# Chunk 2's first layer by half products, chunk 1's second layer in two-bank running sums, and one written order from chunk 0's tail on

## The chip, the cores and the metric

The kernel runs on one core of a Trainium2 chip. Five engines work side by side, each on its own list of instructions: PE (TensorE, matmuls into PSUM), DVE (VectorE) and ACT (ScalarE), which read and write PSUM and SBUF, POOL (GpSimd, SBUF alone), and SP (SyncE), which issues most DMAs. The metric is device time in microseconds; smaller is better. Times of the kernel before are three runs, 273.68 to 274.18, median 273.87.

## The reference

An attention without softmax feeds a layer with an activation. For each of 8 batches and 8 heads, with 576 positions and 64 features:

```python
def phi(x, c, s):                      # c, s: cos and sin of (pi/2) * pos / S
    r = np.maximum(x, 0.0)
    return np.concatenate([r * c, r * s], axis=-1)
q_p, k_p = phi(q, cos_w, sin_w), phi(k, cos_w, sin_w)
kv  = einsum('bhsf,bhsd->bhfd', k_p, v)
num = einsum('bhsf,bhfd->bhsd', q_p, kv)
den = einsum('bhsf,bhf->bhs', q_p, k_p.sum(axis=2))[..., None] + 1e-6
x   = (num / den) as 4608 tokens x 512
h   = x @ w_in                         # 512 x 2048
out = (h / (1 + exp(-beta * h))) @ w_out   # 2048 x 512, fp32
```

Inputs and output are fp32 in HBM; the matmuls take bf16.

## The kernel before

**Tiles and stages.** The 4608 tokens are nine chunks of 512 (eight blocks of 64); the attention comes in eight batches of nine blocks, so batch 2, say, fills chunk 2's last six blocks and chunk 3's first three. For each batch: `load_raw` (L79, on SP) brings q, k and v, 1.15 MB each, into one buffer per name, so that a load waits until the batch before has been read. `q_relu`, `k_relu` (L193 on DVE or L192 on ACT) and `v_scale` (L219 on DVE or L217 on ACT; nine instructions each for cos and for sin) make bf16 operands. `q_turn_dma` (L259) turns q by a DMA on SP, and `tan_mul` (L223, DVE or POOL) makes its sine half. `kv_mm` (L276) and `kv_take` (L286) make kv; `num_all` (L297) makes num for three blocks; `x_div` (L308, L312, L319, all DVE) divides; `x_turn_dma` (L367, SP) turns x into the chunk's `xt`.

**First layer (h).** It has 16 groups of 128 features. `h_group` is four wide matmuls (512 columns, L386) into one bank, and a Silu on ACT (L394) that writes bf16 `g_t`. Chunks 0, 1 and 2 do this. From chunk 3 on, `h_pair` takes two groups at a time as a 2x2 block product with seven half-size products instead of eight (Winograd's form): each product is two narrow matmuls (256 columns, L511) with sums of weights (`wh_sum`, L443) or of x (`x_sum`, L455) as operands. `fast_ops` keeps running sums in two halves of two PSUM banks: a seed copy on ACT (L480), a kept copy (L484, ACT or DVE) and adds on DVE (L487); Silu is L420.

**Second layer (output).** Chunk 0 takes `o_mm`: 64 wide matmuls (L544), four copies (L550), stores by POOL (L537). Chunk 1 takes `o_fast` (L563): seven products of eight narrow matmuls for each half of the tokens, three banks a half, copies L602 to L604 and L582 on ACT, adds L606 to L608 on DVE. Chunks 2 to 8 take `o_pair` (L621), the same seven products through `fast_ops`. The operands are the sums S1 to S4 of `g_t` (`g_sum`, L406, DVE) and T1 to T4 of w_out (`w_sums`, L876 to L879, DVE, 128x2048 each).

**What sets the order.** `manual_schedule` is on: each engine runs its instructions in the order in which the code emits them, and waits by semaphores. Chunk 0, its 32 slots and the work hung into them (`early`), chunk 1 and the first layer of chunk 2 (`h_first`) are loops and lines in the code; from chunk 2's second layer on the order is a string per chunk, `ORDERS`, one word an instruction or a small group (for example `h25` is product 5 of pair 2, `oxd` a kept copy of the output's half x, `s21` a g sum, `w4` a scale on DVE, `v4` one on ACT).

**Around the change.** Slot 27 is the twelfth of chunk 0's sixteen output slots; loads of batch 2 are issued in slot 24. After slot 31, chunk 1's loop (16 `h_group`s) carries `num_rest`, ReLUs, scales and the kv of batch 2 and `w_sums`; then come lines with `o_fast`, batch 2's num in one block (`for t, bank in enumerate((4, 6, 0)): num_all(2, t, bank)`) between the first product of each half and the rest; then `h_first(2)` with batch 3's work and eight w_in sums, and `chunk(2)`.

Of the kernel before, what the change touches and what calls it, by code (L numbers as in the profile page):

```python
# [22 lines left out]
def kernel(  # L23
# [384 lines left out]
    def g_sums(c, i0, i1):  # L408
        for kind in (1, 3, 2, 4):
            got = g_sum(c, i0, i1, kind)  # L410
        return got
# [10 lines left out]
    def wx_tiles():  # L422

        wx["w"] = stage.tile([P, 4, 512], FP32, name="w_stage", tag="w_stage").rearrange("q a f -> q (a f)").bitcast(
            BF16).rearrange("q (k s g f) -> q k s g f", k=4, s=4, g=2)
        wx["v"] = stage.tile([P, 4, 512], FP32, name="w_stage", tag="w_stage").rearrange("q a f -> q (a f)").bitcast(
            BF16).rearrange("q (k s g f) -> q k s g f", k=4, s=4, g=2)
        wx["x"] = stage.tile([P, 4, 512], FP32, name="w_stage", tag="w_stage").rearrange("q a f -> q (a f)").bitcast(
            BF16).rearrange("q (s n c) -> q s n c", s=8, n=NB // 2)
        wx["q"] = stage.tile([P, 4, 512], FP32, name="w_stage", tag="w_stage").rearrange("q a f -> q (a f)").bitcast(  # L430
            BF16)[:, 0 : 2 * NQ * P].rearrange("q (s n c) -> q s n c", s=2, n=NQ)

    def w_sum(jt, i):
        return wx["w" if jt % 4 == 0 else "v"][:, jt // 4, i]

    def wh_sum(jt, kind):
        f0 = jt % 4
        A11, A12, A21, A22 = (win[jt // 4][:, 2 * jp : 2 * jp + 2, f * P : (f + 1) * P]
                              for f in (f0, f0 + 1) for jp in range(2))
        s1, s2, s3, s4 = (w_sum(jt, i) for i in range(4))  # L440
        o, l, r, op = {1: (s1, A21, A22, ALU.add), 2: (s2, s1, A11, ALU.subtract),
                       3: (s3, A11, A21, ALU.subtract), 4: (s4, A12, s2, ALU.subtract)}[kind]
        return nc.vector.tensor_tensor(o, l, r, op=op)  # L443

    def wh_sums(jt):
        for kind in (1, 3, 2, 4):
            got = wh_sum(jt, kind)
        return got
# [55 lines left out]
    def h_pair(c, i):  # L504
# [16 lines left out]
        s1, s2, s3, s4 = (w_sum(jt0, k_) for k_ in range(4))  # L521
# [269 lines left out]
    def second():  # L791
# [22 lines left out]
        28: lambda: x_turn_pe(1, 0, 7, 4, ("act",), (0,)),  # L814
        29: lambda: x_turn_pe(1, 0, 7, 5, ("dve",), (1,)),
    }

    def num_rest():
        for n in range(7, NQ):
            for jp in range(2):  # L820
                num_mm(1, n, jp, 2, 2 * (n - 7) + jp)
        x_mul(x_rden(2, 0, 7, NQ, (0, 1)), 7, NQ)
        x_turn_dma(1, 7, NQ)

    def att_q(b, turn=True):
        q_relu(b, 0)
        q_relu(b, 1)
        if turn:
            q_turn_dma(b)
        if b + 1 < B and b != 3:  # L830
            load_raw(b + 1, "q")

    def v_half(b, cs, n0=0, n1=NQ, eng="dve"):
        if b >= B:
            return
        v_scale(b, cs, n0=n0, n1=n1, eng=eng)
        if cs == 1 and n1 == NQ and b + 1 < B:
            load_raw(b + 1, "v")

    def k_all(b):  # L840
        k_relu(b)
        if b + 1 < B:
            load_raw(b + 1, "k")

    def kv_all(b, bank=6, eng="dve"):
        kv_mm(b, 0, bank)
        kv_mm(b, 1, bank)
        kv_take((0, 1), bank, eng)
# [5 lines left out]
    for slot in range(32):  # L854
# [26 lines left out]
    wx_tiles()  # L881
    for slot in range(16):
        h_group(1, slot)
        if slot == 0:
            num_rest()
            att_q(2)
            v_half(2, 0)
        if 2 <= slot < 6:
            v_half(2, 1, slot + 3, slot + 4, "act")
        if slot == 4:  # L890
            k_all(2)
            v_half(2, 1, 0, 5)
        elif slot == 6:
            w_sums()
        elif slot == 10:
            kv_all(2, eng="act")
            for jp in range(2):
                tan_mul(nc.vector, qs_of(2)[:, jp], qts[0][:, jp], 0, NQ)
    q_relu(3, 0, "act")
    q_relu(3, 1, "act")  # L900
    q_turn_dma(3)

    def one_sums(kind):
        for i0 in range(0, JT // 2, 2):
            g_sum(1, i0, i0 + 2, kind)

    def ops(of, names):
        for n in names.split():
            of[n]()

    x, y = o_fast(1, 0, (2, 5, 4)), o_fast(1, 1, (3, 7, 6))
    ops(x, "1 c1")
    one_sums(1)
    ops(y, "1 c1")
    for t, bank in enumerate((4, 6, 0)):
        num_all(2, t, bank)
    one_sums(2)
    x_part(2, 0, 4)
    ops(x, "6 cu")
    ops(y, "6 cu")  # L920
    one_sums(3)
    ops(x, "2 5 c5")
    x_part(2, 1, 6)
    ops(x, "7")
    one_sums(4)
    ops(x, "a2 a7")
    ops(y, "7 2")
    got = wh_sums(0)
    x_part(2, 2, 0)
    load_raw(4, "q")  # L930
    q_tan(3, 0, got)
    q_tan(3, 1)
    ops(y, "a2 5 c5")
    ops(x, "3 a3 4 c4")
    ops(y, "a7 3 a3 4 c4")
    v_half(3, 0)

    ORDERS = {
        2: (
            "ox16 W61 N12 N00 oy17 x0 oxc4 oyc5 ox5 ox6 oxd k2 k0 k3 k1 v5 x1 N20 oxe W62 oy6 v4 v1 v3 oy5 Lk x2 oyD "  # L940
            "oye v0 ox7 q1 q0 w2 w8 ox3 ox2 oy3 w1 w3 oy7 w7 oy2 v7 w5 w6 oyf w4 oxf oy4 v8 W64 ox4 oyX W63 v6 oyB w0 "
            "t1 t3 t2 v2 oxA t4 Lv Lq oxB"),
        3: (
            "W51 h012 TQ h213 K00 h2c5 W11 h0c7 K1 h22 kT h05 h25 h06 h26 h0d h02 h2d W31 h110 h15 h311 h1c4 h0e h35 "
            "h2e W12 h07 W13 h0f W32 h27 h03 h1d h3d h2f h3c6 h23 h0A W52 h2A h12 W14 h04 W71 h36 W33 W72 h24 h16 h517 "
            "h1e W34 h0B h32 h3e h615 h2B h55 h13 h712 h75 h5D h37 h1A h33 h5c3 h3f h17 h3A h7D h65 h52 h1f h7c4 h6D "
            "g0 h34 h56 h5e h416 W54 W73 h3B h14 h6c1 h76 h72 h1B h45 h53 h4c0 W53 h4d h62 W74 h57 h66 h7e h73 h5A h6e "
            "h5f h77 g1 h42 h7A v7 h46 h7f h4e h67 h63 h54 h6f w2 h74 h6A h47 h43 h4A N03 h64 h5B oy11 h7B h4f h6B h44 "
            "ox10 h4B s11 s30 w4 x0 w6 s10 oyc7 N13 N25 s13 oxc2 s12 s20 v6 v8 k0 ox5 oxd s22 k3 ox2 oy5 w5 v1 s21 k1 "
            "s23 s32 ox6 v2 v3 x1 s31 oxe oyd s42 s40 s41 oy2 oy6 s43 w8 w3 ox3 s33 oye ox7 oy3 q1 v4 v0 w1 w7 k2 Lk "  # L950
            "w0 oy7 oxf v5 oyf ox4 t1 oy4 x2 oxB Lv oyY oxA q0 Lq t2 oyA t4 t3"),
# [38 lines left out]
            "oy6 oy2 oxd s42 s43 s41 oxe s40 oye ox3 oxA ox7 oxf oy7 oyU oyf ox4 oxY oy4 oy3 oyB oyV"),  # L990
    }

    def chunk(c, last):
        b = c + 1
        pairs = {f"h{i}": h_pair(c, i) for i in range(JT // 2)} if c > 2 else {}
        pairs.update({"ox": o_pair(c, 0), "oy": o_pair(c, 1)})
# [95 lines left out]
```

## Time and profile before

| what | value |
|---|---|
| median of 3 runs | 273.87 us (273.68 to 274.18) |
| span of the profiled execution | 272.7 us |
| median less span | 1.2 us |
| PE / DVE / ACT / POOL busy | 97% / 82% / 69% / 25% of the span |
| matmuls | 3712 |
| HBM read and written | 36.71 MB and 9.44 MB |

The page takes one execution. "Busy" adds up the time in which an engine has an instruction in flight; for PE, matmuls overlap, so the distance from one start to the next tells more than the duration (a 256-column matmul lasts 272 ns in its row and the next one starts 109 ns later). The same holds for DVE and ACT to a lesser degree (an add lasts 428 ns and the next starts 336 ns after it). "Idle before" is time in which an engine stood still ahead of a group, with what ended it.

Where the stages lie, by the PE timeline and the chain: chunk 0's second layer 31.9 to 50.4 us (with batch 1's kv and num), chunk 1's first layer to 66 us, its second to 80.6 us, chunk 2's first layer to 95.7 us, its second to 109.7 us; from then on a chunk takes some 27.5 us while batches are in work and 24.5 us without. In four stretches the engines are busy as follows:

| stretch, us | PE | DVE | ACT | POOL |
|---|---|---|---|---|
| 47.5 to 69.0 (21.5) | 21.50 | 17.57 | 16.86 | 4.74 |
| 69.0 to 80.6 (11.6) | 10.64 | 10.11 | 3.23 | 4.09 |
| 80.6 to 95.7 (15.1) | 15.10 | 14.13 | 11.96 | 7.17 |
| 95.7 to 109.7 (14.0) | 14.00 | 12.40 | 8.22 | 0.46 |

### The profile page before, as it was taken

The page shows a single profiled execution, that of the slowest core. Times are in us where ns is not written, and L with a number is a line of the kernel's source. Part 1 is how long each engine was busy: PE and PEld are TensorE (multiplying, and loading weights), DVE is VectorE, ACT ScalarE, POOL GpSimd, SP SyncE. Part 2 cuts the span into 40 slices and gives each one's busy share as a digit, 9 for nine tenths or more (in the row PEclk, how much of TensorE's full clock was granted, in tenths as well). Part 3 has the DMA queues.
Part 4 walks back from the last instruction along what each step waited for, and adds up shares of the span by engine and source line. Part 5 has one row for each costly group of instructions (what it writes and reads, how often), then busy time and mean ns, then how long its engine had stood idle before and what let it go on. Part 6 is the DMA issues. An engine that isn't in the chain of part 4 may idle for free.

```text
span 272.7 us, 8970 instructions
## 1 busy us (share of the span) xinstructions
PE 265.3 (97%) x3712; PEld 206.8 (76%) x3712; DVE 224.0 (82%) x596; ACT 188.4 (69%) x384; POOL 68.3 (25%) x89
## 2 busy tenths in 40 slices
PE   8899999999899999999999999999999999999994
PEld 8554455455784588888888888888888888888883
DVE  5989969499989889789989997899589768757852
ACT  4778777796419656899489966996696179428920
POOL 1444000510078000660085009300840060000001
PEclk9999999999999999999999999999999999999999
DMA  6999999999969999994589439943600570015005
GB/s 237 374 395 383 392 390 319 379 201 336 284 130 311 240 348 226 240 313 103 147 216 370 92 58 223 332 71 62 181 2 2 61 185 1 2 27 130 0 2 155
DMA packets 50681, 54.00 MB, mean 198 GB/s; under 512 B 31232, under 2 KB 31760, under 8 KB 50640
## 3 DMA queue, kind: packets, MB, share of 16 engines
q1 hardware_dynamic: 47504, 45.55, 59.1%
q0 software_dynamic: 2784, 7.61, 9.6%
q8 instruction: 29, 0.48, 0.7%
q10 hardware_dynamic: 352, 0.27, 0.4%
q14 instruction: 12, 0.10, 0.1%
HBM read 36.71 MB, written 9.44 MB: 169 GB/s over the span
## 4 chain that ended last, share of the span: by engine, by line
PE 85%; DVE 9%; DMA 3%; SPq 1%; issue 1%; ACT 1%; DVEq 0%
PE ps L621 32%; PE ps L511 27%; PE ps L386 10%; PE ps L544 5%; PE ps L563 4%; PE ps L297 3%; DMA raw_v<-in_v_dram 3%; PE ps L276 3%; DVE vb L219 1%; DVE xs L319 1%; DVE qs L223 1%; SPq L79 1%; DVE S L406 1%; DVE rk L193 1%; DVE qb L193 0%
## 5 line engine op out<-in xcount | busy, mean ns | idle before, releaser
L537 POOL DMA_DIRECT2D out_dram<-o_sb x58 | 33.9, 591 | 147.3 <-ACT o_sb L658 86.3
L420 ACT ACTIVATE g_t<-ps,beta 128x512 bf16<-128x512 f32 x96 | 60.3, 702 | 1.4 <-PE ps L511 1.3
L621 PEld LDWEIGHTS <-S 128*128 128x128 bf16 x448 | 43.4, 98 | 5.2
L511 PE MATMUL ps<-w_stage 128*128 128x256 bf16 x288 | 46.6, 272 | 0.1
L386 PE MATMUL ps<-xt,win 128*128 128x512 bf16 (+1 forms) x196 | 42.8, 375 | 0.1
L511 PEld LDWEIGHTS <-w_stage 128*128 128x128 bf16 x384 | 37.3, 98 | 5.1 <-issue 0.2
L487 DVE TENSOR_TENSOR ps<-ps,p 128x256 f32<-128x256 f32 x74 | 30.5, 428 | 8.6 <-PE ps L511 3.0
L394 ACT ACTIVATE g_t<-ps,beta 128x512 bf16<-128x512 f32 x48 | 32.3, 688 | 7.2 <-PE ps L386 7.1
L621 PEld LDWEIGHTS <-g_t 128*128 128x128 bf16 x336 | 32.3, 98 | 4.5 <-ACT g_t L420 0.4
L386 PEld LDWEIGHTS <-win 128*128 128x128 bf16 x196 | 18.7, 98 | 21.1 <-issue 0.5
L511 PE MATMUL ps<-xt,win 128*128 128x256 bf16 x192 | 32.9, 273 | 0.0
L511 PEld LDWEIGHTS <-win 128*128 128x128 bf16 x288 | 28.0, 98 | 3.4
L621 PE MATMUL ps<-wout,g_t 128*128 128x256 bf16 x224 | 28.9, 273 | 0.0
L406 DVE TENSOR_TENSOR S<-g_t 128x512 bf16<-128x512 bf16 (+1 forms) x66 | 25.7, 418 | 3.3 <-ACT g_t L420 1.7
L480 ACT COPY ps<-ps 128x256 f32<-128x256 f32 x62 | 22.6, 383 | 7.5 <-PE ps L621 4.0
L217 ACT ACTIVATE vb<-raw_v,sin 128x256 bf16<-128x256 f32 (+1 forms) x58 | 26.0, 503 | 1.5 <-DMA raw_v<-in_v_dram 1.5
L621 PE MATMUL ps<-T,S 128*128 128x256 bf16 x224 | 26.6, 273 | 0.0
L621 PE MATMUL ps<-wout,S 128*128 128x256 bf16 x224 | 26.4, 273 | 0.0
L319 DVE TENSOR_TENSOR xs<-ps,rden 128x768 bf16<-128x768 f32 (+4 forms) x26 | 22.8, 884 | 0.9 <-DVE rden L312 0.2
L223 POOL TENSOR_TENSOR qs<-qt,tanr 128x1152 bf16<-128x1152 bf16 x6 | 14.3, 2387 | 27.4 <-PE ps L563 21.0
L658 ACT COPY o_sb<-ps 128x512 f32<-128x512 f32 x11 | 6.3, 587 | 20.1 <-PE ps L621 20.1
L487 DVE TENSOR_TENSOR ps<-ps,u 128x256 f32<-128x256 f32 x36 | 15.3, 427 | 5.3 <-PE ps L511 3.3
(112 smaller groups left out, 414.7 us busy)
## 6 DMA issues: line engine op xcount, KB each, us to landing
raw_v<-in_v_dram SPq DMA_DIRECT2D x7, 1152.0 KB, 9.7
raw_k<-in_k_dram SPq DMA_DIRECT2D x7, 1152.0 KB, 9.5
raw_q<-in_q_dram SPq DMA_DIRECT2D x7, 1152.0 KB, 7.4
out_dram<-o_sb POOLq DMA_DIRECT2D x58, 128.0 KB, 4.5
w_stage<-in_moe_w_in_dram SPq DMA_DIRECT2D x3, 1024.0 KB, 12.8
w_stage<-in_moe_w_out_dram SPq DMA_DIRECT2D x2, 1024.0 KB, 7.9
w_stage<-in_moe_w_out_dram SPq DMA_DIRECT2D x4, 512.0 KB, 11.9
out_dram<-o_sb SPq DMA_DIRECT2D x10, 128.0 KB, 2.4
```

What stands on the lines that cost most here:

```text
L217: got = nc.scalar.activation(o, a, AF.Copy, scale=t[:, n : n + 1])
L223: return eng.tensor_tensor(dst.rearrange("q n (g p) -> q n g p", g=2), src.rearrange("q n (g p) -> q n g p", g=2), tanr[:, n0:n1].unsqueez ...
L319: nc.vector.tensor_tensor(o.rearrange("q j n s d -> q j (n s) d"), nv[:, :, a:z, :, 0:D].rearrange("q j n s d -> q j (n s) d"), rden[:, :, ...
L386: nc.tensor.matmul(ps[:, h_bank(c, jt), i * 64 : (i + w) * 64], lhsT=win[jt // 4][:, mi, (jt % 4) * P : (jt % 4 + 1) * P], rhs=xt[:, i : i ...
L394: return nc.scalar.activation(gs[c, jt // 4][:, jt % 4], ps[:, h_bank(c, jt)], AF.Silu, scale=beta[:, jt : jt + 1])
L406: return nc.vector.tensor_tensor(o, l, r, op=op)
L420: return nc.scalar.activation(gs[c, jt // 4][:, jt % 4], bank, AF.Silu, scale=beta[:, jt : jt + 1])
L480: return nc.scalar.copy(at("a", 0), at("b", 0))
L487: nc.vector.tensor_tensor(dst, at("b", 0), st["p5"], op=ALU.add)
L511: nc.tensor.matmul(dst, lhsT=l[:, g], rhs=r[:, :, g * HP : (g + 1) * HP], start=start and g == 0, stop=g == 1, skip_group_check=True)
L537: (eng or own).dma_start(out=out_v[bb, n][:, m0:m1], in_=o_sb[hf * HP : (hf + 1) * HP, m0:m1])
L621: nc.tensor.matmul(dst, lhsT=l(i), rhs=r[:, i], start=start and i == 0, stop=i == order[-1], skip_group_check=True)
```

## The change

It has five parts. (1) Chunk 2's first layer is done with `h_pair`, like that of the later chunks; the x sums of chunk 2 are made for it. (2) Chunk 1's second layer is done with `o_pair` instead of `o_fast`. (3) The w_in sums are made for both pairs of a group of four features at once, 16 instructions of 128x512 instead of 32 of 128x256, from chunk 0's tail to chunk 2's first layer. (4) The loops and lines from slot 27 of chunk 0 on are gone; everything from there to the last chunk is one written order. A word may be taken ahead or left for later over a chunk's border: `1/q0@2` in chunk 0's string is chunk 1's word `q0`, for batch 2. (5) Within it, batch work is spread anew over DVE and ACT: `w`, `u` scale by cos and sin on DVE, `z`, `v` on ACT; `q`, `l` are ReLUs on DVE, `r`, `k` on ACT. The orders of chunks 3 to 6 are new too. Chunk 8's is as it was, and chunk 7's too, but for chunk 6's last words at its head.

```diff
-    def wx_tiles():
+    def wx_tiles(names):
...
-        A11, A12, A21, A22 = (win[jt // 4][:, 2 * jp : 2 * jp + 2, f * P : (f + 1) * P]
-                              for f in (f0, f0 + 1) for jp in range(2))
-        s1, s2, s3, s4 = (w_sum(jt, i) for i in range(4))
+        A11, A12, A21, A22 = (
+            win[sl][:, 2 * jp : 2 * jp + 2].rearrange("q g (u r f) -> q g u r f", u=2, r=2)[:, :, :, r]
+            for r in range(2) for jp in range(2))
+        s1, s2, s3, s4 = (w_sum(sl, i) for i in range(4))
...
-        28: lambda: x_turn_pe(1, 0, 7, 4, ("act",), (0,)),
-        29: lambda: x_turn_pe(1, 0, 7, 5, ("dve",), (1,)),
...
-    for slot in range(32):
+    for slot in range(27):
...
-    wx_tiles()
-    for slot in range(16):
-        h_group(1, slot)
-        if slot == 0:
-            num_rest()
-            att_q(2)
-            v_half(2, 0)
...
-    x, y = o_fast(1, 0, (2, 5, 4)), o_fast(1, 1, (3, 7, 6))
-    ops(x, "1 c1")
-    one_sums(1)
-    ops(y, "1 c1")
-    for t, bank in enumerate((4, 6, 0)):
-        num_all(2, t, bank)
...
+    def w_out_sum(kind):
+        z = ALU.subtract
+        o, l, r = {1: (T1, B12, B11), 2: (T2, B22, T1), 3: (T4, B21, T2), 4: (T3, B22, B12)}[kind]
+        return nc.vector.tensor_tensor(o, l, r, op=z)
+
     ORDERS = {
+        0: (
+            "Xwv Sb Sc 1/M1 R0 Sd 1/q0@2 R1 1/u0@2 Se 1/M2 W21 1/r1@2 1/w2@2 1/TQ@2 Sf W22 1/z3@2"),
+        1: (
+            "G7 0/W31 z5@2 0/W01 Z6 G6 M4 kk@2 w0@2 v5@2 G9 G8 Ga u3@2 0/W11 v2@2 G3 G0 Gc z4@2 Gb w6@2 G5 v6@2 u4@2 "
+            "v8@2 G2 u1@2 Lq@3 v7@2 w8@2 w1@2 w7@2 G4 0/W03 y1 Gf y0 Ge Gd G1 K04 s11 K1 oy17 0/W23 Lv@3 kT s12 N03 s33 "
+            "s21 N15 s32 s31 ox12 oyc0 r1@3 s13 Lk@3 s22 s30 oxc1 s10 r0@3 x0 oy5 v6 ox5 x1 z8 TQ v5 Lq@4 N24 z1 v2 oy2 "
+            "oxd s23 s20 oy6 ox2 x2 s43 w3 s41 s40 Xxq oyd l1 oye 0/W32 ox6 oxe 0/W12 t1 w5"),
         2: (
+            "h113 1/oy7 1/ox7 1/s42 1/oyf h15 h014 1/u8 1/v1 1/z7 1/z2 1/k3 1/k0 1/u7 1/w0 1/ox3 1/z4 1/oy3 1/v0 1/z6 "
...
-    def h_first(c):
...
-    h_first(2)
     held = None
-    for c in range(2, NTC):
-        held = chunk(c, held)
+    for c in range(NTC):
+        for op in ORDERS[c].split():
+            other, slash, rest_ = op.partition("/")
+            held = do(int(other), rest_, held) if slash else do(c, op, held)
```

In the new order, `Sb` to `Sf` are chunk 0's output slots 27 to 31, `R0` and `R1` the two turns of x on PE with their copies (ACT, DVE), `G7` an `h_group` of chunk 1, `Z6` `num_rest` into bank 6, `M1` to `M4` the sums T1, T2, T4 and T3 of w_out, `W21` the first w_in sum of the third four features, `y1` a `tan_mul` on DVE, `g1` one on POOL, `kk` the whole k ReLU on DVE, `K0` and `K1` the two kv parts, `kT` the copy of kv on ACT, `N03` num of the first three blocks into banks 3 and 4, `x0` its division and turn, `TQ` the q turn, and `Lq@3` the load of batch 3's q.

## Prediction

> **What bounds the kernel now.** I read the page from the top, then the matmul rows, the PE timeline around its one hole, and the DMA view of batch 2's loads. Page 1 gives the busy shares, page 2 the 40 slices, page 4 the chain that ended last:
>
> ```profile
> PE 265.3 (97%) x3712; PEld 206.8 (76%) x3712; DVE 224.0 (82%) x596; ACT 188.4 (69%) x384; POOL 68.3 (25%) x89
> ...
> PE   8899999999899999999999999999999999999994
> ...
> DVE  5989969499989889789989997899589768757852
> ...
> PE 85%; DVE 9%; DMA 3%; SPq 1%; issue 1%; ACT 1%; DVEq 0%
> ```
>
> TensorE (PE) is full from about 16 us to 269 us, and 85% of the chain is PE. A busy PE need not be a fast one, so I took the distance between matmul starts in the trace: 512 columns start every 0.2155 us, 256 columns every 0.109 us, and between 48 and 269 us hardly a distance is longer. The groups say the same: 188 wide and 8 narrow matmuls of L386 and 672 narrow ones of L511 follow each other with 0.1 us of idle time in all.
>
> ```profile
> L386 PE MATMUL ps<-xt,win 128*128 128x512 bf16 (+1 forms) x196 | 42.8, 375 | 0.1
> L487 DVE TENSOR_TENSOR ps<-ps,p 128x256 f32<-128x256 f32 x74 | 30.5, 428 | 8.6 <-PE ps L511 3.0 <-ACT p L484 2.4 <-ACT kv L286 1.1
> ```
>
> The one real hole stands in chunk 1's output, where the first block of the second product group waits for a copy behind two 1.1 us ReLUs on ACT:
>
> ```profile
> 68.97 0.22 PE L297 MATMUL ps<-kv,qs 64*64 64x65 bf16 x4
> 70.15 1.91 PE L563 MATMUL ps<-T,S 128*128 128x256 bf16 x16 [0.96 <-ACT p L602]
> ```
>
> So the end moves by what PE has to do, by that hole, and by the new waits that PE gets. The profiled execution has a span of 272.7 us; the median of the runs shown is 273.87, 1.2 us around it, and I keep that 1.2 us.
>
> **The change part by part.**
>
> *Chunk 2's h by half products.* 16 groups of 4 wide matmuls go: 64 x 0.2155 = 13.79 us. 8 pairs of 7 products of 2 narrow ones come: 112 x 0.109 = 12.21. **-1.57 us** of PE. The 48 extra weight loads (98 ns each in their rows) lie beside matmuls that start every 109 ns, as they do in the 672 rows of L511; without that cover they would cost 48 x 0.098 = 4.7.
> The Trainium skill, "TensorE: Matmul & The Clock Gate", Back-to-back issue gap, speaks against this step: it says that in a stream of weight loads and matmuls, spacing is about 131 ns at 512 columns and 81 ns at 128. By that, 64 wide ones would take 8.4 us, and 112 narrow ones 11.0 at 98 ns (an estimate between that page's two figures): a loss of 2.6 us. The rows (215.5 and 109 ns) disagree, and agree with the same section's isolated gap, N/2.4 + 2.5 ns.
>
> *The hole at 69 us.* In the new order ACT's first copy of chunk 1's output stands directly behind its product and other products lie between. The step from a num block to a product costs 0.12 elsewhere (97.44 to 97.57); 1.15 - 0.12 = **-1.03**. Next in line there is the DVE chain below.
>
> *Chunk 1's output in two-bank sums.* 112 narrow matmuls before (L563), 112 after: 0. But batch 2's num groups, one block of three before, become a block of two and a single one. A single one cost 0.67 (100.20 to 100.87), two 1.07 (96.56 to 97.63), so a block's own cost is 0.27: **+0.27**.
>
> *Work on DVE and ACT.* By distances between starts (add or copy 0.336, scale 0.262, q ReLU 0.67, sum of 512 0.335): DVE gets 14 adds (+4.7), 13 copies of partial sums (+4.4), whole-bank output copies (+1.1) and 4 x sums (+1.3); it loses 7 q ReLUs (-4.7), 11 scales (-2.9), and 32 w_in sums of 0.202 become 16 of 0.335 (-1.1). Net about +3. ACT gets 11 scales of 0.40 (+4.4) and 7 q ReLUs of 1.07 (+7.5): about +11.6, on an engine busy 69%. Both cost nothing while PE covers them. From slot 27 to the end of chunk 2's output (75 us of PE work) DVE has 66 us in the old order and some 70 in the new: still under PE, with little play. So the waits have to be looked at one by one.
>
> *Batch 2's ReLUs and scales, moved ahead.* They read loads that the change doesn't move:
>
> ```profile
> raw_q<-in_q_dram SPq DMA_DIRECT2D x1, 1152.0 KB, 7.4
> raw_v<-in_v_dram SPq DMA_DIRECT2D x1, 1152.0 KB, 11.5
> raw_k<-in_k_dram SPq DMA_DIRECT2D x1, 1152.0 KB, 13.8
> ```
>
> Issued at 40.40, 40.83 and 41.43, they land at 47.8, 52.33 and 55.3. DVE ends chunk 0's last multiply at 47.45; then come T1 (1.14), q ReLU (0.67), the xt copy (0.61), and at 49.9 the scale u0, which waits for raw_v until 52.4. Behind it on DVE stand T2, four w_in sums and the division of batch 1's last blocks: 0.26 + 1.14 + 0.34 + 0.26 + 3 x 0.34 + 0.20 + 0.26 + 0.69 = 4.15, so the division's end reaches PE at 56.58. PE begins chunk 1's h at 50.36 as before; at 0.862 a group it comes to its fifth (bank 4, behind the second's Silu) at 54.29 and to its seventh (bank 6, behind that division) at about 56.2. On ACT the scale z3 waits for raw_v too; z3, Silu, z5 and a Silu of 0.69 end at 54.44, so the fifth group waits **0.20** and the seventh **0.37**: **+0.57**. Further on DVE runs without a wait to the division ahead of the single num group: 18.2 us of work, done at 70.7, where PE comes at 70.95. Nothing more is lost there, by 0.2 us.
> Bounds: if raw_v were early enough, 0; each us that it lands later is a us of PE.
>
> *The q turn, moved ahead on SP.* It is now issued at about 49.7 instead of 55.47, behind batch 2's loads while they run, and batch 1's last xt turn and batch 3's loads stand behind it on SP. The trace has this case later:
>
> ```profile
> 109.69 0.37 SPq L79 DMA_DIRECT2D raw_v<-in_v_dram  x1
> 110.12 1.50 SPq L79 DMA_DIRECT2D raw_q<-in_q_dram  x1
> 111.73 11.25 SPq L259 DMA_TRANSPOSE qt<-qb  x1
> ```
>
> The turn holds SP until 122.98, and raw_q lands at 122.93, 6.1 us behind raw_v, where the three issued from 60.21 on, with a turn only 8 us later, landed 2.9 us apart (67.51, 70.37, 73.33). So the load just ahead of the turn may be 3 us late (it is raw_k here, needed at 57.5, with 2.2 us to spare), and SP is held to about 56: batch 3's q lands by about 65, its ReLU is due at 67. Nothing lost; bounds 0 and the 3.2 us of a raw_v that is as late. I take 0, as the load two ahead of a turn (raw_v at 109.69) took 7.1, the least of its row.
> The Trainium skill, "DMA: Bandwidth & Descriptors", Queues, rings and completion order, says that an issuing engine's descriptors are consumed in ring order on each DMA engine, which would leave raw_v alone; these rows agree for that load, and not for the one next to the turn.
>
> *Shorter distances.* I counted, for each matmul that waits for a DVE add or an ACT copy, the PE work between the product that feeds it and itself. Before, the shortest is 8 matmuls, 0.87 us. In the new order 16 adds have 6, 0.65 us. The round trip, from the trace: last matmul's start to add's start 0.31 at the least, add 0.423, add's end to PE 0.05 (171.42 to 171.48): 0.784, against 0.654 + 0.109 = 0.763. So 0.02 each if DVE is free; if a 0.335 sum has just begun, 0.36. **+0.45** for the 16 (0.028 each, nearest to the free case, since the order leaves DVE a slot there), bounds 0.3 and 5.7.
>
> Sum: -1.57 - 1.03 + 0.27 + 0.57 + 0.45 = **-1.31 us**; span 271.4, time **272.5**.
>
> **The rivals.**
> *A, the forecast*, 272.1 to 273.0.
> *B, no wait is left*: raw_v lands earlier or the adds fit. -1.57 - 1.03 + 0.27 = -2.33, and the 0.24 wait at 171.13 goes too: 271.3. For it: from 100 us on such an order has waits of under 0.3 us a chunk. Against: u0 and z3 stand ahead of the work PE needs.
> *C, slower: the q turn holds raw_v back.* Place: DVE's u0 and ACT's z3. Price: the whole delay, as nothing else is ready. At 1.3 us the gain is used up, at 1.9 it is slower by over 0.2%; the 3.2 us that raw_q lost at 110 give 275.7. For it: that row, and stores from 50.8 on. Against: raw_v is not next to the turn.
> *D, the short distances cost what a DVE behind its work costs*: 0.1 to 0.13 each, 1.6 to 2.1 us: 273.7 to 274.1, no change. For it: DVE has 70 us in 75. Against: the sums can be late without harm.
> *E, two narrow matmuls with two loads cost more than a wide one with one*: the 48 loads uncovered, +4.7, 277.2. Against: 672 rows of L511 at 109 ns. The matmul rule of the skill, above, points this way. That the change doesn't do what it says is left out: the new program has 64 wide matmuls fewer and 112 narrow ones more.
>
> **How the numbers follow.** A 0.46, B 0.20, C 0.14, D 0.19, E 0.01. The range takes in B and D and the start of C: 271.1 to 274.4. About 0.2%, 0.55 us, is what a measurement of this kernel can tell from no change. Faster (under 273.3): A, B and the mild end of D, 0.71. Within: most of D and the start of C, 0.15. Slower: the rest of C, E, and a worse D, 0.14.
>
> **What would show it.** L386 with 64 wide matmuls fewer; the 0.96 before T,S gone; DVE and ACT idle for raw_v until about 52.4 and a PE wait of some 0.2 and 0.4 us between 54 and 57; h pairs of chunk 2 in about 12.3 us without long gaps; after some 112 us the chunks as long as before. Wrong would be: raw_v landing after 53.6; PE waits for L478's adds of over 0.1 us each; a new wait for batch 3's raw_q or raw_v on ACT around 67 to 72; a hole ahead of the single num group at about 71.

## The result, and the profile after

The kernel after takes **281.9 us** (median of 6 runs, 281.1 to 286.9) beside 273.98 for the kernel before (6 runs, 273.4 to 275.4): a ratio of 1.028, 95% interval 1.026 to 1.031. It is 7.9 us slower, where 272.5 was forecast and 271.1 to 274.4 was the range. The profiled execution has a span of 281.0 us against 272.7: 8.3 us to be found. (The intervals leave disturbed runs out; the medians and ranges are of all runs.)

Of the page of the kernel after, these rows answer to those shown of before (busy shares, slices, chain by engine):

```profile
PE 266.7 (95%) x3756; PEld 210.8 (75%) x3760; DVE 230.8 (82%) x594; ACT 200.5 (71%) x403; POOL 65.6 (23%) x89
...
PE   8899999998699999999987999999999999999994
...
PE 64%; DMA 22%; DVE 6%; ACT 4%; issue 1%; SPq 1%; ACTq 0%; DVEq 0%
```

PE is busy for 1.4 us more in a span that is 8.3 us longer, so most of the loss is PE standing idle (a stand), not work. The slices say where: the 8 and the 6 lie at 63 to 77 us (slices of 7.0 us), the 8 and the 7 at 141 to 155. And the chain has changed its kind: 22% of it is now DMA, 3% before. In the chain of the kernel after, between 45 and 82 us, this piece is new (start, us, what):

```profile
49.83 16.75 DMA qt<-qb
66.58 0.02 issue
66.60 2.63 DVE qs L223 x2
```

The q turn that the change issues earlier, at 49.83 instead of 55.47, is on its way for 16.75 us and lands at 66.58. Before, it was on its way for 6.7 and landed at 62.17. The eight output stores beside it are late as well: issued from 51.02 to 54.82, they land at 63.34 to 66.80, where the run e3 below has them land at 56.19 to 58.33. The DVE timeline shows who meets it (start, us, what, and in brackets the idle time ahead and its releaser):

```profile
61.93 0.42 DVE L439 TENSOR_TENSOR w_stage<-win 128x512 bf16<-128x512 bf16 x1
66.60 2.63 DVE L223 TENSOR_TENSOR qs<-qt,tanr 128x1152 bf16<-128x1152 bf16 x2 [4.25 <-DMA qt<-qb]
```

DVE stands for 4.25 us at the tan multiply, with the g sums and the divisions of batch 2 queued behind it, and then PE meets the missing operands one after another. PE timeline from 68 to 80 us:

```profile
69.28 0.23 PE L297 MATMUL ps<-kv,qs 64*64 64x65 bf16 x4 [0.98 <-DVE qs L223]
...
72.97 1.92 PE L612 MATMUL ps<-T,S 128*128 128x256 bf16 x16 [1.74 <-DVE S L406]
...
75.64 0.22 PE L297 MATMUL ps<-kv,qt 64*64 64x65 bf16 x2 [0.59 <-DVE xs L319]
```

The brackets count from the modelled end of the matmul before. By starts, as in the prediction, the four delays are 1.19, 1.90, 0.80 and (at 79.8) 0.19: **4.08 us**. Two chunks on, a second place costs nearly as much. PE, DVE and POOL timelines from 144 to 151 us:

```profile
146.44 0.38 PE L502 MATMUL ps<-xt,w_stage 128*128 128x256 bf16 x2 [0.64 <-DVE ps L478]
...
150.82 0.38 PE L502 MATMUL ps<-w_stage,win 128*128 128x256 bf16 x2 [1.58 <-DVE ps L478]
```
```profile
143.91 0.62 DVE L219 TENSOR_SCALAR vb<-raw_v,cos 128x256 bf16<-128x256 f32 x2 [1.74 <-DMA raw_v<-in_v_dram]
...
147.63 2.80 DVE L219 TENSOR_SCALAR vb<-raw_v,sin 128x256 bf16<-128x256 f32 x2
```
```profile
147.62 2.39 POOL L223 TENSOR_TENSOR qs<-qt,tanr 128x1152 bf16<-128x1152 bf16 x1
```

In chunk 4 the scales of batch 6 wait for a load (1.74 us on DVE, 0.97 on ACT), and PE loses 0.40, 0.47 and 0.80 at 144 to 146. Then two scales that take 0.61 us elsewhere take 2.80, exactly while POOL's tan multiply runs, and PE loses 1.74.

All of it by distances between starts: products and block work -1.57 + 0.27, the two old waits -1.03 and -0.24, a later start of chunk 1 +0.22 (50.36 to 50.58), chunk 1's first layer +0.99, the q turn +4.08, a load in chunk 3 +0.59, loads in chunk 4 +1.67, POOL beside DVE +1.74, waits of less than 0.2 us behind 80 us +1.95 (30 waits of 2.71 us against 10 of 0.57, less the 0.19 above). That is 8.7, 0.4 more than the spans show; the 0.4 is not assigned.

### The profile page after: what moved, and what is told of

Read it like the earlier page. It is cut to its first block, busy times and chain, and to the rows that moved or that the text cites. A ratio compares the mean times of both kernels' runs of the same rounds, so it can differ in the third digit from the quotient of the medians.

```text
span 281.0 us, 9101 instructions
## 1 busy us (share of the span) xinstructions
PE 266.7 (95%) x3756; PEld 210.8 (75%) x3760; DVE 230.8 (82%) x594; ACT 200.5 (71%) x403; POOL 65.6 (23%) x89
## 4 chain that ended last, share of the span: by engine, by line
PE 64%; DMA 22%; DVE 6%; ACT 4%; issue 1%; SPq 1%; ACTq 0%; DVEq 0%
PE ps L612 29%; PE ps L502 28%; DMA raw_v<-in_v_dram 8%; DMA qt<-qb 6%; DMA raw_q<-in_q_dram 5%; PE ps L297 3%; DMA raw_k<-in_k_dram 3%; PE ps L386 2%; PE ps L276 2%; DVE S L406 1%; DVE xs L319 1%; ACT vb L217 1%; SPq L79 1%; DVE qs L223 1%; ACT rk L192 1%
## 5 line engine op out<-in xcount | busy, mean ns | idle before, releaser
L612 PEld LDWEIGHTS <-S 128*128 128x128 bf16 x512 | 49.6, 98 | 8.4 <-DVE S L406 2.2
L502 PE MATMUL ps<-w_stage 128*128 128x256 bf16 x336 | 54.4, 272 | 0.6 <-ACT ps L471 0.6
L502 PEld LDWEIGHTS <-w_stage 128*128 128x128 bf16 x448 | 43.6, 97 | 8.7 <-issue 2.1
L478 DVE TENSOR_TENSOR ps<-ps,p 128x256 f32<-128x256 f32 x85 | 34.9, 427 | 6.8 <-PE ps L502 4.7
L502 PE MATMUL ps<-xt,win 128*128 128x256 bf16 x224 | 39.1, 273 | 0.0
L612 PE MATMUL ps<-wout,S 128*128 128x256 bf16 x256 | 31.1, 273 | 0.0
L386 PE MATMUL ps<-xt,win 128*128 128x512 bf16 (+1 forms) x132 | 29.0, 372 | 0.7 <-DVE xs L319 0.3
L406 DVE TENSOR_TENSOR S<-g_t 128x512 bf16<-128x512 bf16 x64 | 25.5, 418 | 0.7 <-ACT g_t L416 0.7
L386 PEld LDWEIGHTS <-win 128*128 128x128 bf16 x132 | 12.6, 98 | 15.3 <-issue 1.7
L223 POOL TENSOR_TENSOR qs<-qt,tanr 128x1152 bf16<-128x1152 bf16 x6 | 14.4, 2396 | 31.9 <-DVE S L406 15.7
L502 PE MATMUL ps<-w_stage,win 128*128 128x256 bf16 x112 | 19.8, 272 | 2.0 <-DVE ps L478 2.0
L502 PE MATMUL ps<-xt,w_stage 128*128 128x256 bf16 x112 | 20.8, 272 | 0.6 <-DVE ps L478 0.6
```

What stands on the lines that cost most here:

```text
L223: return eng.tensor_tensor(dst.rearrange("q n (g p) -> q n g p", g=2), src.rearrange("q n (g p) -> q n g p", g=2), tanr[:, n0:n1].unsqueez ...
L386: nc.tensor.matmul(ps[:, h_bank(c, jt), i * 64 : (i + w) * 64], lhsT=win[jt // 4][:, mi, (jt % 4) * P : (jt % 4 + 1) * P], rhs=xt[:, i : i ...
L478: nc.vector.tensor_tensor(dst, at("b", 0), st["p5"], op=ALU.add)
L502: nc.tensor.matmul(dst, lhsT=l[:, g], rhs=r[:, :, g * HP : (g + 1) * HP], start=start and g == 0, stop=g == 1, skip_group_check=True)
L612: nc.tensor.matmul(dst, lhsT=l(i), rhs=r[:, i], start=start and i == 0, stop=i == order[-1], skip_group_check=True)
```

## The experiments

Times are medians, ratios are to the kernel before, measured beside it, and an edit is to the kernel after unless another is named. Four theories go through the expectations. **S**: the q turn's 2304 packets of 256 bytes share the DMA engines with chunk 0's eight output stores (which POOL issues from 51 us on), and that makes it slow. **Q**: the turn waits for the loads issued ahead of it on SP. **P**: POOL's multiply shuts DVE's scale out. **F**: a stand that appeared in the first runs is PE waiting for its own instructions.

### e1: chunk 0's stores behind the turn

```diff
         nc.scalar.copy(o_sb, o_ps)
+        if c == 0:
+            kept.append((tt, o_sb))
+            return
         store(c, tt, o_sb)
...
+        elif k_ == "P":
+            for tt, o_sb in kept:
+                store(0, tt, o_sb, behind=last)
```

The word `Px` stands behind `y1` in chunk 1's string; `behind` makes a store wait for that multiply, so all eight stores start behind the turn (from 64.33 us on).

> The changed kernel, with chunk 0's eight stores issued only once batch 2's q turn has been read (by the first of its two tan multiplies on DVE). In the changed kernel that turn lands at 66.58, 10.4 us behind the load ahead of it, DVE idles 4.25 us for it, and PE then loses 1.19 + 1.90 + 0.80 + 0.19 = 4.1 us between 68 and 80. Theory S (the turn's 256-byte packets crawl because the stores' 4096-byte packets share the DMA engines with them): the turn lands 2 to 4 us behind raw_k, at 58 to 60, DVE has no wait for it, time about 278 (277.5 to 278.5). Theory Q (it crawls because of where it stands in the queue, behind the loads and ahead of the next xt turn, stores or not): it still lands after 65, time 281.5 to 282.5.

279.86 us, 1.021 (1.016 to 1.025). The turn, issued at 50.09, landed at 59.53, not at 66.58, and DVE came to its multiply without a wait:

```profile
62.01 0.41 DVE L439 TENSOR_TENSOR w_stage<-win 128x512 bf16<-128x512 bf16 x1
62.34 2.61 DVE L223 TENSOR_TENSOR qs<-qt,tanr 128x1152 bf16<-128x1152 bf16 x2
```

S holds, in part: behind raw_k's landing the turn needed 3.5 us (56.03 to 59.53) instead of 10.4 (56.15 to 66.58). The DMA view of the two from raw_k to the turn's landing (queue, packets, MB, share of 16 engines), first after, then e1:

```profile
q1 hardware_dynamic: 2222, 0.69, 67.3%
q0 software_dynamic: 379, 1.03, 50.1%
```
```profile
q1 hardware_dynamic: 2083, 0.52, 115.3%
```

About the same number of the turn's packets, but the stores' 379 took half of the engines' time. The time fell by 2.0 us only, less than the 4.08 that went, because PE now stood for 1.27 us at 71.8: a new stand, taken up below.

### e2: the k load behind the turn

```diff
-            for name in "qvk":
+            for name in "qv":
...
-            "... 1/TQ@2 Sf W22 1/z3@2"),
+            "... 1/TQ@2 1/Lk@2 Sf W22 1/z3@2"),
```

> The changed kernel, with batch 2's raw_k load issued behind the q turn and not ahead of it. Theory Q: the turn lands 2 to 4 us behind raw_v, at 55 to 57, and DVE has no wait for it; time about 278 unless the k ReLU (ready at 58.2) waits for raw_k. Theory S: the turn meets the stores all the same from 53 us on and lands after 60; raw_k, issued at about 53, crawls beside them too and the k ReLU waits for it, 1 to 4 us; time 279 to 283.

285.15 us, 1.038 (1.033 to 1.044). The turn landed at 57.54, 4.8 us behind raw_v (52.74). Neither theory's landing was met, the time is above both forecasts, and the run does not tell S from Q: with nothing but raw_v ahead, most of the turn's packets ran from 51 to 54.3 us, before the stores' came, so the edit took the stores out of its way as well. With e1 it does say that the 16.75 us have two parts: some 6.3 until the load next to it had landed, and 10.4 beside the stores. The k load paid for it: issued at 53.25, landed at 63.50, and DVE waited 5.38 us for it. In chunk 4 PE stood for 2.75 us at 145.6, and from 150.3 to 155.0 its clock was at half.

### e3: the turn where it was; e4: POOL's multiply behind the scales

```diff
-            "... 1/w2@2 1/TQ@2 Sf W22 1/z3@2"),
+            "... 1/w2@2 Sf W22 1/z3@2"),
...
-            "G7 0/W31 z5@2 0/W01 Z6 G6 M4 ..."
+            "G7 0/W31 z5@2 0/W01 Z6 TQ@2 G6 M4 ..."
```

> The changed kernel, with the q turn of batch 2 issued where the kernel before has it, behind batch 1's last xt turn, at about 59 us. Theory S: by then the stores are through (in the kernel before they are by 58), the turn lands at 62 to 63.5, DVE waits 0 to 1.2 us for it, the 4.1 us of PE shrink to 0 to 1; time 278 to 279. Theory Q: the same landing, since no load is ahead of it any more; the two theories differ in the first two runs, and this one gives what the moved word costs. If instead the later loads (batch 3's q and v stand behind the turn) become late, new waits on ACT or DVE appear at 67 to 75 and the time stays above 280.

279.98 us, 1.023 (1.016 to 1.030); the profiled span is 277.7, 3.3 less than after. The turn was issued at 58.46 and landed at 63.08: 4.6 us, against 16.75. Issued 8.6 us later, it is there 3.5 us earlier, and DVE waits 0.81 us for it, as forecast:

```profile
63.10 2.63 DVE L223 TENSOR_TENSOR qs<-qt,tanr 128x1152 bf16<-128x1152 bf16 x2 [0.81 <-DMA qt<-qb]
```

The time, forecast at 278 to 279, was not met: PE stands again at 71.7, for 1.29 us.

```diff
-            "... 3/Lk h13 h12 h07 3/Lq g0 "
-            "h35 v1 h27 h1A h0f u2 h3c1 u0 h17 ..."
+            "... 3/Lk h13 h12 h07 3/Lq "
+            "h35 v1 h27 h1A h0f u2 h3c1 u0 g0 h17 ..."
```

> The changed kernel, with one tan multiply on POOL (chunk 4's first) put behind the two DVE scales u2 and u0 that it overlaps at 147.6 to 150.0. Theory P (DVE's scale, SBUF to SBUF, stands still while POOL's multiply runs: 2540 ns instead of 343): the scale takes 0.35, PE's 1.74 wait at 149 goes, time 280.2 (279.9 to 280.6). Theory L (the late raw_v load of batch 6, landed at 143.88, costs this time and the multiply only stands beside it): the wait stays or moves, time 281.5 to 282.2.

280.83 us, 1.026 (1.019 to 1.033); span 278.5. The two scales, in the DVE timeline of e4 at the place where they took 2.80:

```profile
146.99 0.61 DVE L219 TENSOR_SCALAR vb<-raw_v,sin 128x256 bf16<-128x256 f32 x2
```

The wait of 1.74 us on PE is gone and nothing takes its place; the waits for raw_v ahead of it remain. P holds. The times alone would not show it, nor what e3 gains: the intervals of e3 and e4 both overlap that of the kernel after (1.026 to 1.031), and only e1's (1.016 to 1.025) lies clear of it. For e3 and e4 the traces decide.

### The stand at 71 us

In e3 the first product of batch 2's single num block shows this in the PE timeline, and DVE this:

```profile
71.68 0.22 PE L297 MATMUL ps<-kv,qt 64*64 64x65 bf16 x2
72.98 0.22 PE L297 MATMUL ps<-kv,qt 64*64 64x65 bf16 x2 [1.08 <-DVE S L406]
```
```profile
71.12 0.96 DVE L319 TENSOR_TENSOR xs<-ps,rden 128x768 bf16<-128x768 f32 x1
72.00 0.75 DVE L406 TENSOR_TENSOR S<-S,g_t 128x512 bf16<-128x512 bf16 x2
```

What the num block needs is the division, which ends at 72.08; the view names the g sum beside it. But PE goes on only at 72.98, 0.9 us behind the division (1.47 in e1). In the kernel after, at the same third matmul, the division ends at 75.60 and PE goes on at 75.64. PE's own instructions (matmuls, weight loads, waits), counted from 0 in the trace's order, make the place a border. Every stand that no semaphore explains, in e1, in this run and in all later ones, ends at instruction 189 to 193 of a block of 256, whatever the work is there: at 449 (f4, g1), 705 and 1469 (e7), 1214 (e8), 1981 (e1, e3 and every run from e6 on), 2749 and 6333 (f4). The expectation of g1 counts 15 fewer and calls 1981 instruction 1966. The trace has 29 packets of 16 KB of the queue "instruction", and PE goes on 1.3 to 1.6 us behind the landing of one of them. That is theory F; e7, f4 and g1 test it.

### e6: both edits, and the load ahead of the last turns of x

e3 and e4 together; chunk 3's string has `d0` (the division alone) for `x0`, and `Lv D0` (batch 6's load of v, then the turn of x) behind `z1`, where `Lv` stood at the end.

> Three edits of the changed kernel at once: the q turn in its old place (as in e3), the POOL multiply behind u2 and u0 (as in e4), and in chunk 3 the load of batch 6's raw_v issued ahead of the xt turn of the first num block and not behind it. In e3 PE still waits 0.13 + 0.47 + 0.79 + 1.74 us between 141 and 148. Theory L (the first three come from raw_v, which lands at 140.71 there because SP issues it at 134.4, behind two xt turns, while its buffer is free from about 131.6): it is issued 2 to 3 us earlier, lands by 138.5, and all four waits go: e3's 279.98 - 3.1 = 276.9 (276.3 to 277.5). Rival A (ACT, which is packed from 121 to 137 us in the changed kernel, is late by itself): the 0.47 and 0.79 stay, 278.2.

280.39 us, 1.022 (1.019 to 1.025); a miss. The load came earlier (issued 132.26, landed 139.16, not 143.88), but the two turns of x issued right behind it landed only behind it, at 139.87 and 140.52. The DVE and PE timelines of e6:

```profile
139.97 0.43 DVE L446 TENSOR_TENSOR w_stage<-xt 128x512 bf16<-128x512 bf16 x1 [3.66 <-DMA xt<-xs]
```
```profile
140.44 0.38 PE L502 MATMUL ps<-w_stage 128*128 128x256 bf16 x2 [2.53 <-DVE w_stage L446]
```

A turn next behind a load landed only behind that load here, as the q turn did in e1 and e2 (3.5 and 4.8 us behind); this time it was the x sums that PE needed. PE's clock was at half from 141.2 to 144.2 behind it.

### e7 and e8: borders moved, leads made longer, both on e6

```diff
-    warm_pe(58, 48)
+    warm_pe(116, 24)
```

Twice as many of the empty matmuls that start PE, half as wide: the same time, 58 more matmuls on PE's list (with their weight loads), so that every border falls on other work.

> e6 with the 58 warm-up matmuls of 48 columns at the very start made 116 of 24 columns: no more time, but 116 PE instructions more ahead of everything. In e3 PE stands 1.29 us in front of the single num group at 71.7; the DVE semaphore it waits for came at 72.09, it went on at 72.98, 1.5 us after a 16 KB packet of the instruction queue had landed (e1: semaphore 71.63, on at 73.09, also 1.5 us behind such a packet). Theory F (PE has run out of code there: the fetch is late because the num blocks and kv products use up instructions fast): with the code's block borders 116 instructions earlier the stand at 71.7 shrinks to what DVE explains (0.4) or moves elsewhere; time 0.5 to 1.0 under e6's, or equal if it comes back at another place. Rival N (it belongs to the num group itself or to a wait that the trace doesn't show): it stays at 71.7 with 1.2 to 1.5 us, time as e6.

285.35 us, 1.037 (1.034 to 1.041). The stand at 71.8 is gone; others are there. Two have no semaphore (releaser "issue") and lie in the middle of batch work: 2.61 us at 16.3 and 3.08 at 70.7. One of 1.24 at 50.1 lies ahead of a turn of x; the view names a q ReLU on DVE, but the division that the turn needs had ended at 49.61. F holds, and the edit costs more than what it was meant to remove.

e8 is e6 with nine words each moved by one product, so that an add has 8 matmuls and not 6 between the product that feeds it and the one that waits, such as

```diff
-            "... h1A h17 h36 h03 h2e h35 h1f ..."
+            "... h1A h17 h36 h2e h35 h03 h1f ..."
```

> e6 with nine h products each moved by one product (2 matmuls) so that a matmul that waits for a DVE add, or the product that feeds it, has 8 matmuls between instead of 6. In the changed kernel an add with two semaphore waits starts 0.379 us behind its product's last matmul start (0.310 with one wait) and PE loses 0.102 at each of some ten places with 6 between. Theory D (the round trip is 0.866 us, and 8 x 0.109 = 0.872 covers it): eight or nine of the 0.102 waits go, time 0.8 to 0.9 under e6's, about 276.1. Rival (DVE is late anyway, and the add only starts as late as before): the waits stay and the time is e6's.

282.73 us, 1.029 (1.026 to 1.033): inconclusive in the time. The waits of about 0.1 us fell from 11 (in e3) to 6, but one code packet lay beside batch 2's three loads and took 3.87 us (42.83 to 46.70), and PE stood 2.29 us at 46.0 behind it; the 3.43 at 142.1 are e6's wait for the turns of x again.

### f1, f2, f3: scales behind their loads, then the leads

f1 is e3 and e4 together, and chunk 4's six early scales of batch 6 moved some 2.6 us back:

```diff
-            "... h1c1 h25 w7 w0 h2D u8 h05 "
-            "h0d h16 3/ox4 3/ox3 w5 z3 h1D h0c7 3/t4 3/oxB h1e h2c2 v4 h06 3/oxA h26 h0e h2e 3/Lk h13 h12 h07 3/Lq g0 "
+            "... h1c1 h25 h2D h05 "
+            "h0d h16 3/ox4 3/ox3 h1D h0c7 3/t4 3/oxB h1e h2c2 h06 3/oxA h26 h0e h2e w7 w0 z3 3/Lk h13 u8 h12 v4 h07 w5 3/Lq "
```

> The changed kernel with the q turn in its old place (as e3), the POOL multiply behind u2 and u0 (as e4), and chunk 4's first six scales (w7, w0, u8 on DVE, z3, v4 on ACT, w5) moved some 2.6 us of PE work further back, so that they stand behind the landing of batch 6's raw_v and not ahead of it. Theory L (in-order engines: DVE and ACT stand at the first of these scales until raw_v lands at 140.7, with copies and adds that PE needs behind them): of e3's 0.13 + 0.47 + 0.79 + 1.74 us between 141 and 148 nothing over 0.2 is left; time 276.4 at full clock (276.0 to 277.0). Rival A (ACT is late by itself there): waits of 0.4 to 0.8 stay, 277.7.

279.73 us (277.4 to 281.8), 1.018 (1.012 to 1.024), span 275.6. The median is above what either theory expected (276.4 and 277.7); the profiled run, 277.41, is the quickest of the six. In its trace the waits of 0.13, 0.47, 0.79 and 1.74 that e3 has at 141 to 148 us are gone; one of 0.84 at 143.3 is new, where the moved scales stand together in front of an add. The stand at 71.5 is 1.71.

f2 is f1 with batch 2's first scales behind other work in the same way: `1/u0@2 1/w2@2` at the end of chunk 0's string, `z3@2 z5@2` behind `G6` in chunk 1's.

> f1, and the first two scales that wait for batch 2's raw_v (u0 on DVE, z3 on ACT, with w2 and z5 behind them) put behind work that doesn't need raw_v. In e3 PE waits 0.35 at chunk 1's fifth h group and 0.45 at the seventh for them. Theory: both go, time 0.7 to 0.9 under f1's. Rival: the engines only stand later, at 53, and a later group waits; time as f1.

277.23 us, 1.014 (1.008 to 1.019), span 275.2. The two waits of chunk 1's first layer (0.44 and 0.45 in f1) are gone. The span falls by only 0.4 us; the medians differ by 2.5, more than these waits explain, and the intervals overlap.

f3 is f2 with the nine longer leads.

> f2 with nine h products moved by one product, so that 8 matmuls and not 6 lie in the round trip over a DVE add (as in e8, whose trace has 6 waits of 0.10 us left of 11). Theory D (round trip 0.866 us, 8 x 0.109 = 0.872 covers it): five to eight waits of 0.10 us fewer, time 0.5 to 0.8 under f2's. Rival: the adds only start later by as much, no change.

276.36 us (10 runs), 1.009 (1.006 to 1.013), span 273.9. Waits of about 0.1 us: 6 instead of 11. Its interval overlaps that of f2, so the times alone do not settle what the leads are worth; the traces show 0.5 us of waits less. PE's longest waits in the kernel after and in f3 (us in total, times, longest), without those of the first 15 us:

```profile
PE ps L502 <- DVE ps L478: 2.6, 3, 1.6
PE ps L612 <- DVE S L406: 1.7, 1, 1.7
...
PE ps L297 <- DVE qs L223: 1.0, 1, 1.0
```
```profile
PE ps L502 <- DVE ps L478: 0.8, 1, 0.8
PE ps L297 <- DVE S L406: 0.6, 1, 0.6
```

f3 is the best version found, 5.5 us under the kernel after by the medians (7.1 by the profiled spans; f3's profiled run is the quickest of its ten), and it is still slower than the kernel before. No version that beats both was found. What it keeps: 0.84 at 70.6, 0.94 at 142.8, and 23 waits under 0.2 us behind 80 us (2.29 us in all, 0.57 before).

### f4 and g1: fewer early matmuls, after and before

f4 is f3 with `warm_pe(29, 96)`; g1 is the **kernel before** with `warm_pe(43, 65)`: 15 empty matmuls and their weight loads fewer, some 30 instructions, in the same time, and nothing else.

> f3 with 29 warm-up matmuls of 96 columns at the start and not 58 of 48: the same time, 58 PE instructions fewer ahead of everything, so the borders of the 16 KB code blocks fall 58 instructions later in the work. Theory F (the 1.0 to 1.3 us in front of the single num group at 71.5 are a code block that comes late; with 116 instructions more, in e7, it moved into the middle of a num block as 3.08 us): the stand at 71.5 goes or changes its size and place by more than 0.5 us, and wherever PE stands with no semaphore to wait for, it goes on 1.4 to 1.5 us behind the landing of a 16 KB packet of the instruction queue. If it goes, time 1.0 to 1.3 under f3's. Rival N (it belongs to the single num group): it stays at 71.5 with 1.0 to 1.3.

284.04 us, 1.035 (1.030 to 1.040). Stands of 1.8 to 2.0 us at 15.4, 73.8 and 102.3 have no semaphore, and each is at a border; so is one of 0.8 at 218.4. A fourth, of 1.8 at 178.7, is of another kind: PE waits for a copy on ACT, and that one through DVE for a load of raw_v.

> The kernel before the change, with 43 warm-up matmuls of 65 columns at the start and not 58 of 48: the same time, 30 PE instructions fewer ahead of everything, nothing else. In the kernel before, PE passes its instructions 1710 and 1966 (the two borders of 16 KB code blocks around the three num groups) at 66.1 and 68.7 us and doesn't stand; with 30 fewer the borders fall 30 instructions later in the work, at 67.8 and 68.9. Theory F (each block is fetched when the border before it is passed and is there 2.5 us later at the least): PE stands in the num groups at its instruction 1966 for 1.4 us or more, and goes on 1.3 to 1.6 us behind the landing of a 16 KB packet; up to 1.0 us of it is taken from the 0.96 hole right behind; time 274.2 to 276.9, middle 275.5. Rival N (the stands in the changed kernels belong to their single num group, or to waits that the trace doesn't show): no stand, 273.8 as before.

281.72 us, 1.029 (1.025 to 1.033). This kernel differs from the one before by 15 empty matmuls at its head, and loses as much as the whole change. At the border that the kernel before passes at 68.70 without a stand (the packet ahead of it had landed at 66.3), PE now has its longest one. PE timeline of g1, in batch 2's num:

```profile
71.97 0.22 PE L297 MATMUL ps<-kv,qt 64*64 64x65 bf16 x2
75.45 0.22 PE L297 MATMUL ps<-kv,qt 64*64 64x65 bf16 x2 [3.26 <-issue]
```

A 16 KB packet had landed at 74.15, 1.3 us ahead.

And a few us later its table of stretches (window; busy time and instructions of PE, PEld, DVE, ACT, POOL; granted clock; DMA share; GB/s):

```profile
74.00:77.00 3.00, 1.55 (x26) 1.38 (x27) 2.93 (x9) 0.21 (x1) 0.00 (x0) 0.99 1.31 158
77.00:80.00 3.00, 3.00 (x16) 2.07 (x15) 0.87 (x4) 0.53 (x2) 0.00 (x0) 0.50 1.13 144
```

At a clock of 0.50 PE starts 16 matmuls in 3 us, where it starts 30 before. The same pair, 2.74 us of standing and then half clock, lies at 14.4 us. The stand is where F put it; the expectation, 274.2 to 276.9, was too low because it had one stand and no half clock.

## Why the prediction was wrong, step by step

**The step that failed is "the q turn, moved ahead on SP", taken at 0.** I saw that a turn next behind a load may hold things up, looked for the harm in the loads around it (SP held until 56, raw_k 3 us late, rival C's raw_v), and bounded it by those. I never asked when the turn itself would land, nor for whom: by its old row, 6.7 us from issue to landing, it seemed early by far. The trace of before already spoke against that. Over its six q turns, the view of L259 gives

```profile
DMA to landing us min/median/max: 5.6/11.3/14.3
```

and the turn at 111.73, whose row the prediction shows, took 13.2. With 13.2 a turn issued at 49.7 lands at 62.9, and in the kernel after DVE is ready for it at 62.35 (66.60 less the 4.25 that it stands). So the step had a price by the trace of before, though even 14.3 would give only some 1.7 of the 4.25. The runs show 16.75: 6.3 until raw_k's load had landed, then 10.4 beside eight stores (e1: 3.5 without them). DVE, in order, stood 4.25 us in front of it, PE lost 4.08. In its old place (e3) it takes 4.6 and is there earlier. It is the largest term of the miss, 4.08 of 9.6 us (-1.3 forecast, +8.3 found), but not the only one: without it, in e3, the kernel is still slower than before.

**"Both cost nothing while PE covers them" (work on DVE and ACT) failed next.** The totals were nearly right (DVE 230.8 busy, ACT 200.5, against 224.0 and 188.4: +6.8, of which 2.2 are the two blocked scales, and +12.1, where 3 and 11.6 were worked out; the terms of the second, 4.4 and 7.5, add up to 11.9), but I walked the queues one by one only around batch 2. Scales in chunks 3 and 4 that now stand in front of PE's adds and copies wait for raw_v: 0.59 and 1.67 us (the latter gone in f1, where they stand later, for a new one of 0.84). Another ran into POOL: 1.74 (e4: gone). The trace of before had the sign, a scale of 1107 ns beside POOL's multiply at about 80 us where others take 343, and the prediction made no use of it. The Trainium skill, "SBUF — State Buffer", Who interferes with whom, says that DVE and GpSimd share one pair of ports, that an instruction which takes it holds it to its end, and that the other engine is fully blocked meanwhile. By that rule a scale that needs the pair, and meets POOL's multiply there, waits for all of it; the trace agrees, 2.80 us for two scales next to POOL's 2.39, and e4's 0.61.

**Shorter distances: right mechanism, wrong size.** Taken at 0.45 (0.028 each); the small waits behind 80 us grew by about 2 us. Ten of them, 0.10 each, are of this kind; the others were not followed one by one. The sum is what rival D said (1.6 to 2.1), but D had another reason, a DVE behind its work, so that its figure came out is luck. The term that was mis-sized is the round trip: 0.784, from one add that has a single semaphore to wait for. Most adds that wait for two, with the program's separate wait ahead of them, start 0.379 us behind the product's last matmul instead of 0.310: 12 of the 14 in the kernel after that PE's matmul releases. The trace of before has this too, for 9 of 14; the prediction took the least. So the round trip is 0.379 + 0.433 + 0.054 = 0.866 us, 0.10 more than the 0.763 that 6 matmuls cover. That is what 10 places show, for instance at 117.26 in the PE timeline of after:

```profile
116.94 0.38 PE L502 MATMUL ps<-xt,w_stage 128*128 128x256 bf16 x2
117.26 0.38 PE L502 MATMUL ps<-xt,win 128*128 128x256 bf16 x2
117.47 0.38 PE L502 MATMUL ps<-xt,w_stage 128*128 128x256 bf16 x2
```

0.32 where two narrow matmuls take 0.22. At places with one semaphore it is 0.03, as worked out.

**Batch 2's ReLUs and scales: right mechanism, wrong size.** Forecast: the fifth group 0.20 late and the seventh 0.37. Measured: 0.48 and 0.51, 0.99 in all. The chain was as told, but batch 2's loads were issued 0.5 us later (41.30 instead of 40.83 for raw_v), and raw_v landed at 52.86, not 52.33; "each us that it lands later is a us of PE" held. f2 removed it.

**Half products: right.** L386 has 64 matmuls fewer; 256 columns still start every 0.109 us:

```profile
L386 PE MATMUL ps<-xt,win 128*128 128x512 bf16 (+1 forms) x132 | 29.0, 372 | 0.7 <-DVE xs L319 0.3
L502 PE MATMUL ps<-xt,win 128*128 128x256 bf16 x224 | 39.1, 273 | 0.0
```

No idle time lies in front of the new products here, so the weight loads were hidden, and rival E and the Trainium skill's matmul spacing, as the prediction quotes it, are out.

**The hole at 69 us: right and useless.** The 0.96 ahead of T,S is gone, but the same product waits 1.74 for its g sum, because DVE stood before. "A hole ahead of the single num group at about 71" was named as what would show the prediction wrong; it came (0.59 at 75.6 after, and with the turn in time, a border's stand).

**Rival C** had the right culprit with the wrong victim: raw_v was hardly held back (0.5 us, all of it from its later issue), and the price fell on the turn itself.

**What could not be seen in the source or the trace of before** is the stand at the borders. In the kernel after it costs nothing by itself, since PE stands there anyway; it takes part of what e1 and e3 give back. So the expected 1.3 us were there (f3 still has the shorter products), and were paid away to one late transfer, four waits behind loads and POOL, and leads that are 0.1 us too short. In f3, with the first two repaired, 1.2 us of span over the kernel before is left (2.5 by the medians): the leads and two waits of some 0.9 us use up more than the shorter products give. Whether a full order without those would beat the kernel before was not tried.

Two small slips in the prediction's sums change nothing: the row of terms ahead of batch 1's last division adds up to 4.17, not 4.15, and 273.87 - 1.31 is 272.56.

## What to carry to other kernels

When a transfer is moved ahead, work out its landing anew: list what is on the queue in front of it and which other streams its packets will meet, and do not carry one old duration along: the same kind of transfer may take two or three times as long elsewhere in the trace. When work is spread over in-order engines, walk every queue for a load, or a port that another engine holds, in front of the critical engine's next operand; a share of busy time (DVE 82% before and after) says nothing of it. And a running sum needs a lead of the full round trip with the number of semaphores that it really waits for.

## What the runs showed of the hardware

- **PE can stand for its own instructions.** 29 packets of 16 KB come in during a run (30 in e7). Where PE stands at the border of a block of 256 instructions with no semaphore left to wait for, it goes on 1.3 to 1.6 us behind the landing of one; the stands are 0.8 to 3.5 us long. Num groups, 96 instructions in some 0.5 us, use up a block fastest. Where a border falls depends on the count of all instructions before it: 15 matmuls fewer at the start cost 8 us (g1). A border alone does not make PE stand: in the kernel before, the packet landed at 66.3 and PE passed at 68.70; in e3, at the same count, the packet landed at 71.5 and PE went on at 72.98. What makes a packet late is open: that a block is asked for only once the border before it is passed is my reading of when the packets start, not tested by itself.
- **Half clock after a stand.** Of 14 distances of 1.9 us and more between two starts on PE (behind 12 us, all profiled runs), 9 were followed, 0.7 to 2.2 us behind their end, by 1.3 to 4.7 us (mostly 3) at half clock; no shorter one was. The Trainium skill, "TensorE: Matmul & The Clock Gate", Part 1: The HAM clock gate, has the clock fall to half after at least one idle window of about 3.4 us that runs free. The halving agrees (granted clock 0.50 in g1), as does that it hits only some; but a distance of 2.2 us between two starts was enough in e7; why is not shown.
- **A turn of 256-byte packets** takes 4.6 us from issue to landing with no store beside it (e3), 16.75 behind a load and beside stores (the kernel after); SP, which issued it, was held for 6.71 us of that.
